# Key transposes of the next chunk moved into the visit of the chunk before it

## The chip, the cores and the metric

The program runs on one core of one Trainium2 chip. The metric is the device time of one execution in microseconds; a kernel's time is the median of its runs, and less is better.

## The reference

A gated linear attention (4 batches, 8 heads, 768 positions, 48 channels a head) feeds two feed-forward layers over its 3072 rows of 384 channels. All is float32.

```python
f = 1.0 / (1.0 + np.exp(-f_logit))
for t in range(S):
    state = f[:, :, t, :, None] * state + np.einsum('bhd,bhe->bhde', k[:, :, t], v[:, :, t])
    y[:, :, t] = np.einsum('bhd,bhde->bhe', q[:, :, t], state)
# x: y as 3072 rows of 384 channels
h = np.maximum(x @ w_in, 0.0);  x = h * h @ w_out
h = x @ w_in2;  out = np.where(h > 0, h, np.exp(np.minimum(h, 0)) - 1) @ w_out2
```

## The kernel before

**Chunks.** The attention is cut into 24 chunks: 128 positions of one batch, chunk g being of batch g % 4. Within a chunk the recurrence is replaced by matmuls: running products of the gates (two scans on VectorE, DVE) scale q and k, products of q and k give scores inside the chunk, and a state per batch carries what came before. Four chunks make a block of 512 rows, the unit of the feed-forward layers.

**Slots.** The two layers have 6 blocks each with 16 slices of the hidden width, so 192 units. The program is recorded in slots: in slot u TensorE (PE) gets `up(u)`, nine matmuls of 512 columns into one bank, and `down(u - 2)`, nine matmuls of 512 columns into three banks `y`; `between(u)` gives ScalarE (ACT) and DVE the activation of unit u (on ACT `r` and `gg`, on DVE `gh`), and `low(u)` gives GpSimd (POOL) the subtraction `gl` of 128x512 that follows `gh`. What `down` reads was made nearly two slots earlier. Every 16 slots a block ends: one slot later (slots 33, 49, 65) its three `y` banks are copied out, two of them by DVE and one by ACT.

**Steps of a chunk.** A plan hands each step of chunk g to a slot, and the steps of a slot are recorded ahead of that slot's `up`. Each engine works its own queue strictly in that order. `NEAR[g]` is the slot of chunk g's visit: 19, 21, 23, 25 for chunks 8 to 11, then 28, 32, 36, and so on to 72 for chunk 23. The steps:

- `load_f`, `load_qk`: DMAs from the SP queue of the gates, and of k and q;
- `a_gate`: a tanh on ACT, then a scaling on POOL, on 112x521 gates;
- `a_decay`: on DVE a memset, two scans with a reciprocal between them and a minimum (`mn`); on POOL two operations of 112x4 (`wc`, and up to chunk 19 `dlast`);
- `a_scale`: on DVE q, then k, are multiplied by the products, in place (112x512 each);
- `a_keys`: four PE transposes of k (128x112 outputs) into the bank `a2`; `a_transposed`: ACT copies them to SBUF as `kt`;
- the visit: `a_far(g - 1)` (32 small matmuls of q with the states into the two banks of outputs `a0` and `a1`), `a_near(g)` (64 small matmuls), `a_out(g - 1)` (32 more into the banks of outputs, and ACT's copies of them), then on DVE `a_mask` and `a_states`;
- `a_rows`, `a_hi`, `a_lo`: six small DMAs, then a copy on ACT and the subtraction `xl` on DVE, that make the layer's input of it.

From slot 28 on the weights of the second layer are decoded beside this, once in four slots: in the slot after a visit an ACT copy `dec` and three DVE operations on 128x768 (L58, L61, L62), three slots later a split on ACT and DVE.

The step slots of chunk g were tied to its own visit:

```python
a = NEAR[g]
d = a - (4 if g <= 3 * B else 6)        # B = 4
at(d - 2, load_f, g);  at(d, load_qk, g);  at(d, a_gate, g)
at(d + 1, a_decay, g); at(d + 2, a_scale, g)
for h in (a_keys, a_transposed):
    at(a - (1 if g <= 3 * B else 2), h, g)
```

So for chunk 19, visited in slot 56: gates in slot 50, scans in 51, scaling in 52, transposes in 54.

Of the kernel before, what the change touches and what calls it, by code (L numbers as in the profile page):

```python
# [11 lines left out]
F32 = mybir.dt.float32  # L12
# [5 lines left out]
AF = mybir.ActivationFunctionType  # L18
# [3 lines left out]
B, H, S, D = 4, 8, 768, 48  # L22
NT, DM, DFF = B * S, H * D, 2048
NG = NT // 128
# [3 lines left out]
NP = H // 2  # L28
ROWS = 112
# [11 lines left out]
NEAR = dict(zip(range(B, NG), (5, 7, 9, 11, 19, 21, 23, 25, *range(28, 4 * NG - 23, 4))))  # L41
# [42 lines left out]
def chunked(ctx, tc, ff, qk, vk, vz, wraw, mask, ident, flag, out):  # L84
# [7 lines left out]
    V, A, G, PE = nc.vector, nc.scalar, nc.gpsimd, nc.tensor  # L92

    one = ctx.enter_context(tc.tile_pool(name="one", bufs=1))
# [7 lines left out]
    ps_a = ctx.enter_context(tc.tile_pool(name="ps_a", bufs=1, space=PSUM))  # L102

    idt = one.tile([128, 128], F32, name="idt")
# [18 lines left out]
    st = {}  # L123
# [82 lines left out]
    def a_keys(g):  # L206
        k = st[g]["k"].rearrange("r (p t) -> r p t", p=NP)
        st[g]["tp"] = tp = ps_a.tile([128, NP, 128], F32, tag="a2", name=f"tp{g}")
        for p in range(NP):
            PE.transpose(tp[:, p, 0:ROWS], k[:, p], idt[:ROWS, :ROWS])  # L210

    def a_scores(g):
        s = st[g]
        a_keys(g)
        q, k = (s[n].rearrange("r (p t) -> r p t", p=NP) for n in "qk")
        pool, tags = (ps_h, "hh") if g % 2 else (ps_y, ("y0", "y1"))
        s["sc"] = sc = [pool.tile([128, NP, 128], F32, tag=tags[j], name=f"sc{g}_{j}") for j in range(2)]
        for p in range(NP):
            for j, (lo, hi) in enumerate(HD):
                PE.matmul(sc[j][:, p], k[lo:hi, p], q[lo:hi, p], start=True, stop=True)  # L220
# [63 lines left out]
    def a_far(g):  # L284


        s = st[g]
        q = s["q"].rearrange("r (p t) -> r p t", p=NP)
        s["o"] = o = [ps_a.tile([128, NP, 64], F32, tag=f"a{c}", name=f"o{g}_{c}") for c in range(2)]
        for p in range(NP):  # L290
            for j, n in QUARTERS:
                c = j ^ n
                lo, hi = HD[j]
                PE.matmul(  # L294
                    o[c][64 * n:64 * n + 48, p], (s0, s1)[c][lo:hi, p], q[lo:hi, p, 64 - 64 * c:128 - 64 * c],
                    start=p == 0, stop=False, skip_group_check=True,
                )

        seen = one.tile([128, 2, NP], F32, tag="seen", name=f"seen{g}")
        for c in range(2):  # L300
            A.activation(seen[64:112, c], o[c][64:112, :, 0], AF.Copy)
# [252 lines left out]
    def at(slot, f, *args, to=plan):  # L554

        if slot > 1:
            to.setdefault(slot, []).append((f, args))
# [2 lines left out]
        at(f - 5, load_raw, 0, f)  # L560
    for g in range(B, NG):
        a = NEAR[g]
        d = a - (4 if g <= 3 * B else 6)
        at(d - 2, load_f, g)
        at(d, load_qk, g)
        at(d, a_gate, g)
        at(d + 1, a_decay, g)
        at(d + 2, a_scale, g)
        for h in (a_keys, a_transposed):
            at(a - (1 if g <= 3 * B else 2), h, g)  # L570
        at(d + 1 if g < B + 2 else max(d + 1, NEAR[g - 1] + 1), load_v, g)
        over = g > B and g != 2 * B
        if over:
            at(a, a_far, g - 1)
        at(a, a_near, g)
        if over:
            at(a, a_out, g - 1)
            at(a + 1, a_rows, g - 1)
        at(a, a_mask, g)
        at(a, a_states, g)  # L580
        if g in (2 * B - 1, NG - 1):
            for h in (a_far, a_out):
                at(a + 2, h, g)
            at(a + 3, a_rows, g)
            for h in (a_hi, a_lo):
                at(a + 4, h, g, to=behind)
        else:
            for h in (a_hi, a_lo):
                at(NEAR[g + 1] + 3, h, g)
# [21 lines left out]
    with tc.manual_schedule():  # L611
# [8 lines left out]
        for _ in range(3):  # L620
# [4 lines left out]
            "T": lambda: [nc.sync.dma_start(out=tri[c:c + 64], in_=mask[c:c + 64, 64 - c:128 - c]) for c in (0, 64)],  # L625
            "f": load_f, "q": load_qk, "v": load_v, "r": lambda f: load_raw(0, f),
            "g": a_gate, "d": a_decay, "c": a_scale, "s": a_scores, "t": a_transposed, "m": a_mask, "k": a_state,
            "y": a_direct, "h": a_hi, "l": a_lo,
            "x": a_whole, "b": begin_weights, "w": finish_weights, "C": store_weights,
# [113 lines left out]
@with_exitstack  # L743
def gated_attention_moe(ctx: ExitStack, tc: tile.TileContext, ff, qk, vk, vz, nat, wraw, mask, ident, out):
    pool = ctx.enter_context(tc.tile_pool(name="flag", bufs=1))
    flag = pool.tile([1, 1], I32, name="flag")
    with ExitStack() as inner:
        chunked(inner, tc, ff, qk, vk, vz, wraw, mask, ident, flag, out)
    rv = tc.nc.values_load(flag[0:1, 0:1], min_val=0, max_val=1)
    with tc.If(rv == 1):  # L750
        with ExitStack() as inner:
            general(inner, tc, nat, wraw, ident, out)
# [58 lines left out]
```

## Time and profile before

| | |
|---|---|
| median of 3 runs | 887.52 us (886.96 to 887.74) |
| the profiled execution | 887.76 us, of it 886.0 us span |
| PE busy | 871.9 us, 98% of the span, 6240 matmuls |
| DVE busy | 552.8 us, 62% |
| ACT busy | 454.1 us, 51% |
| POOL busy | 280.7 us, 32% |
| chain of work that ended last | PE 96%, its lines L533 and L469 44% each |
| line of the transposes (L210) in that chain | 1% |

The span is that of the one execution that was profiled; 1.8 us of that execution's time lie outside it. Shares of busy time are means over stages that differ: the first 30 us are the start, up to 480 us the first layer runs with the attention beside it, then the second layer alone. A row of a view by time gives the start in us from the span's start, the duration, the engine, the source line, the operation, and output<-inputs with sizes; "x4" merges equal neighbours, and then the duration is that of all of them.

### The profile page before, as it was taken

The numbers are of one execution on the slowest core, as the hardware profiler recorded it, in microseconds if no ns is written. First come the engines' busy times: TensorE is split into PE (matmuls) and PEld (weight loads), VectorE is DVE, ScalarE is ACT, GpSimd is POOL, SyncE is SP. The second block draws the span as 40 slices with busy tenths as digits, with TensorE's granted clock in tenths as the row PEclk, the third lists the DMA queues.
The fourth block names the chain that finished last, engine by engine and source line by source line (L and its number), as shares of the span: only waits on it lengthen the run. The fifth ranks groups of instructions, "written<-read, shape, count | busy, mean of one in ns | idle before, by whom it ended". The sixth has DMA issues, their size and how long they took to land.

```text
span 886.0 us, 15946 instructions
## 1 busy us (share of the span) xinstructions
PE 871.9 (98%) x6240; PEld 699.8 (79%) x6240; DVE 552.8 (62%) x841; ACT 454.1 (51%) x816; POOL 280.7 (32%) x244
## 2 busy tenths in 40 slices
PE   7999999999999999999999999999999999999996
PEld 5566678888888888888888888888888888888885
DVE  8997578888677777654431555555655654664543
ACT  4877745555544555544544444444544544444543
POOL 2120045443334232322333232333323232332321
PEclk8999999999999999999999999999999999999999
DMA  9994321335444343513686300100100200100001
GB/s 261 351 302 163 101 90 49 118 106 161 147 156 153 115 151 117 182 47 123 229 299 238 131 13 1 59 13 1 60 12 1 66 7 14 58 1 35 2 0 40
DMA packets 36516, 92.40 MB, mean 104 GB/s; under 512 B 5809, under 2 KB 12977, under 8 KB 36433
## 3 DMA queue, kind: packets, MB, share of 16 engines
q1 hardware_dynamic: 36288, 91.18, 30.9%
q8 instruction: 50, 0.82, 0.4%
q14 instruction: 34, 0.27, 0.1%
q10 hardware_dynamic: 144, 0.13, 0.0%
HBM read 64.55 MB, written 22.02 MB: 98 GB/s over the span
## 4 chain that ended last, share of the span: by engine, by line
PE 96%; DVE 1%; DMA 1%; ACT 1%; SPq 0%; issue 0%; ACTq 0%; DVEq 0%
PE y L533 44%; PE ph L469 44%; PE o L294 1%; PE o L309 1%; PE tp L210 1%; PE sk_a L233 1%; DMA vz<-vz 1%; PE yp L278 1%; PE sk_a L242 1%; PE sc L220 0%; PE sk_h L242 0%; PE ph L458 0%; PE sk_h L233 0%; PE kv L268 0%; DVE t L502 0%
## 5 line engine op out<-in xcount | busy, mean ns | idle before, releaser
L516 POOL TENSOR_TENSOR gl<-gg,gh 128x512 fp32r<-128x512 f32 x175 | 233.7, 1336 | 471.4 <-PE ph L469 191.8
L533 PE MATMUL y<-gh,wf 128*128 128x512 f32 (+1 forms) x582 | 178.0, 387 | 0.3 <-ACT yo L545 0.3
L502 DVE SCALAR_TENSOR_TENSOR t<-r,t 128x512 f32<-128x512 f32 (+1 forms) x97 | 72.3, 745 | 154.8 <-ACT r L501 154.6
L498 ACT ACTIVATE r<-ph 128x512 f32<-128x512 f32 (+1 forms) x97 | 57.8, 596 | 181.5 <-PE ph L469 176.6
L469 PE MATMUL ph<-xh,w 128*128 128x512 f32 x558 | 149.7, 403 | 0.8 <-DVE w L430 0.8
L533 PE MATMUL y<-gh,w 128*128 128x512 f32 x480 | 147.8, 389 | 0.0
L469 PE MATMUL ph<-xh,wf 128*128 128x512 f32 (+1 forms) x582 | 146.4, 387 | 0.0
L533 PEld LDWEIGHTS y<-gh,wf 128*128 128x128 f32 x582 | 108.8, 188 | 22.8 <-ACT yo L545 0.5
L469 PEld LDWEIGHTS ph<-xh,wf 128*128 128x128 f32 x582 | 108.6, 188 | 22.3
L469 PEld LDWEIGHTS ph<-xh,w 128*128 128x128 f32 x558 | 101.4, 188 | 24.8 <-DVE w L430 1.4
L533 PE MATMUL y<-gl,wf 128*128 128x512 f32 (+1 forms) x291 | 112.5, 387 | 0.0
L533 PEld LDWEIGHTS y<-gh,w 128*128 128x128 f32 x480 | 90.1, 188 | 18.8
L490 ACT ACTIVATE r<-ph 128x512 f32<-128x512 f32 x80 | 47.8, 598 | 105.8 <-PE ph L469 88.5
L533 PE MATMUL y<-gl,w 128*128 128x512 f32 x240 | 93.4, 389 | 0.0
L469 PE MATMUL ph<-xl,wf 128*128 128x512 f32 (+1 forms) x291 | 81.1, 387 | 0.0
L469 PE MATMUL ph<-xl,w 128*128 128x512 f32 x279 | 78.5, 389 | 0.0
L503 DVE SCALAR_TENSOR_TENSOR gg<-ph,t 128x512 f32<-128x512 f32 (+1 forms) x97 | 66.6, 686 | 10.4 <-DVE t L502 0.5
L496 DVE TENSOR_TENSOR gh<-r 128x512 fp32r<-128x512 f32 x64 | 44.1, 688 | 45.2 <-ACT r L490 44.7
L533 PEld LDWEIGHTS y<-gl,wf 128*128 128x128 f32 x291 | 54.6, 188 | 11.1
L469 PEld LDWEIGHTS ph<-xl,wf 128*128 128x128 f32 x291 | 54.3, 188 | 11.1
L500 ACT ACTIVATE t<-r 128x512 f32<-128x512 f32 (+1 forms) x97 | 61.0, 629 | 3.1
L501 ACT ACTIVATE r<-r 128x512 f32<-128x512 f32 (+1 forms) x97 | 60.9, 628 | 3.1
(110 smaller groups left out, 1054.7 us busy)
## 6 DMA issues: line engine op xcount, KB each, us to landing
raw<-wraw SPq DMA_DIRECT2D x32, 768.0 KB, 6.9
wst<-w SPq DMA_DIRECT2D x16, 768.0 KB, 3.4
wf<-wst SPq DMA_DIRECT2D x16, 768.0 KB, 4.7
ff<-ff SPq DMA_DIRECT2D x22, 227.9 KB, 6.3
k<-qk SPq DMA_DIRECT2D x22, 224.0 KB, 3.4
q<-qk SPq DMA_DIRECT2D x22, 224.0 KB, 4.5
x2d<-yo SPq DMA_DIRECT2D x18, 256.0 KB, 2.7
x<-x2d SPq DMA_DIRECT2D x18, 256.0 KB, 3.0
```

Source lines behind the costliest of these rows:

```text
L210: PE.transpose(tp[:, p, 0:ROWS], k[:, p], idt[:ROWS, :ROWS])
L233: PE.matmul(sc[j][64 * c:64 * c + 64, p], k[lo:hi, p, 64 * c:64 * c + 64], q[lo:hi, p, 64 - 64 * c:128 - 64 * c], start=True, stop=True,)
L469: PE.matmul(ph, w[:, a, 0, 128 * k:128 * k + 128], b[:, k, c], start=(m == 0), stop=(m == len(todo) - 1))
L490: A.activation(r[:, c], ph, AF.Relu)
L496: V.tensor_tensor(out=gh[:, c], in0=r[:, c], in1=r[:, c], op=ALU.mult)
L498: A.activation(r[:, c], ph, AF.Relu, scale=-1.0)
L500: A.activation(t[:, c], r[:, c], AF.Tanh, scale=-0.5)
L501: A.activation(r[:, c], r[:, c], AF.Exp, scale=-1.0)
L502: V.scalar_tensor_tensor(out=t[:, c], in0=r[:, c], scalar=1.0, in1=t[:, c], op0=ALU.add, op1=ALU.mult)
L503: V.scalar_tensor_tensor(out=gg[:, c], in0=ph, scalar=0.0, in1=t[:, c], op0=ALU.max, op1=ALU.add)
L516: G.tensor_tensor(out=gl, in0=gg, in1=gh, op=ALU.subtract)
L533: PE.matmul(yp_[i][m][:, c], w[:, 128 * m:128 * m + 128], b[:, c], start=(f == 0 and n_ == 0), stop=(f == NF - 1 and n_ == len(terms) - 1) ...
```

## The change

For chunks 12 to 23 the transposes of k move from two slots ahead of the chunk's own visit (chunk 12: one slot) to the front of the visit of the chunk before it. They are written not to the bank `a2` but to the columns 256 to 479 of the two banks of outputs, which that visit fills in columns 0 to 255. ACT's copy `kt` becomes two copies of half the width, one slot after that visit. The other steps are now tied to that earlier visit: with d = NEAR[g - 1] - 3 the gates are worked in slot d, the scans in d + 1, the scaling in d + 2, in the slot ahead of the transposes. For chunks 13 to 23 each of these comes one slot earlier than before, for chunk 12 two slots. Chunk 19 now has its gates in slot 49, its scans in 50, its scaling in 51 and its transposes in 52. The loads of v, the visits and all feed-forward work keep their slots.

```diff
+    def a_keys_ahead(g):
+        k = st[g]["k"].rearrange("r (p t) -> r p t", p=NP)
+        st[g - 2]["oo"] = oo = [ps_a.tile([128, 512], F32, tag=f"a{c}", name=f"o{g - 2}_{c}") for c in range(2)]
+        st[g]["tp"] = tp = [o[:, 256:480].rearrange("r (p t) -> r p t", p=2) for o in oo]
+        for p in range(NP):
+            PE.transpose(tp[p // 2][:, p % 2], k[:, p], idt[:ROWS, :ROWS])
+
+    def a_transposed_ahead(g):
+        st[g]["kt"] = kt = one.tile([128, NP, ROWS], F32, tag="kt", name=f"kt{g}")
+        for c in range(2):
+            A.activation(kt[:, 2 * c:2 * c + 2], st[g]["tp"][c], AF.Copy)
...
     def a_far(g):
-        s["o"] = o = [ps_a.tile([128, NP, 64], F32, tag=f"a{c}", name=f"o{g}_{c}") for c in range(2)]
+        if "oo" in s:
+            o = [i[:, 0:256].rearrange("r (p t) -> r p t", p=NP) for i in s["oo"]]
+        else:
+            o = [ps_a.tile([128, NP, 64], F32, tag=f"a{c}", name=f"o{g}_{c}") for c in range(2)]
+        s["o"] = o
...
-        d = a - (4 if g <= 3 * B else 6)
+        ahead = g >= 3 * B
+        d = NEAR[g - 1] - 3 if ahead else a - 4
...
-        for h in (a_keys, a_transposed):
-            at(a - (1 if g <= 3 * B else 2), h, g)
+        if ahead:
+            at(d + 4, a_transposed_ahead, g)
+        else:
+            for h in (a_keys, a_transposed):
+                at(a - 1, h, g)
...
+        if g + 1 < NG and g + 1 >= 3 * B:
+            at(a, a_keys_ahead, g + 1)
         if over:
             at(a, a_far, g - 1)
```

PE, chunk 19. Before, the end of slot 53 and the begin of slot 54 (`y3_...` is `down`, `ph3_6` is `up`, `tp19` the transposes):

```order
L533 MATMUL y3_1_3449<-gh3_3_3501,w0_3_457 128x512 x2
L533 MATMUL y3_1_3449<-gl3_3_3502,w0_3_457 128x512
L533 MATMUL y3_2_3450<-gh3_3_3501,w0_3_457 128x512 x2
L533 MATMUL y3_2_3450<-gl3_3_3502,w0_3_457 128x512
L210 MATMUL tp19_3665<-idt_85,k19_3433 128x112 x4
L469 MATMUL ph3_6_0_3678<-xh3_2514,w0_6_612 128x512 x6
L469 MATMUL ph3_6_0_3678<-xl3_2515,w0_6_612 128x512 x3
```

After, the end of slot 51 and the begin of the visit of slot 52 (`o17_0` and `o17_1` are the two banks of outputs, the rows with `q17` are `a_far(17)`):

```order
L550 MATMUL y3_1_3457<-gl3_1_3431,w0_1_416 128x512
L550 MATMUL y3_2_3458<-gh3_1_3430,w0_1_416 128x512 x2
L550 MATMUL y3_2_3458<-gl3_1_3431,w0_1_416 128x512
L218 MATMUL o17_0_3513<-idt_85,k19_3392 128x112 x2
L218 MATMUL o17_1_3514<-idt_85,k19_3392 128x112 x2
L311 MATMUL o17_0_3513<-q17_2921,s0_97 48x64 x2
L311 MATMUL o17_1_3514<-q17_2921,s1_98 48x64 x2
```

The transposes stand between the last matmul of one slot and the first small matmuls of the visit, two slots earlier.

DVE, from the copies of a finished block in slot 49 on (`gh3_1` belongs to slot 49, `gh3_2` to 50, `gh3_3` to 51; `ds1` are the products of chunk 19, and masks with `sk18` belong to the visit of slot 52). Before:

```order
L547 COPY yo2_0_3408<-y2_0_2494 128x512
L547 COPY yo2_2_3414<-y2_2_2496 128x512
L496 TENSOR_TENSOR gh3_1_3417<-r3_1_3419 128x512
L496 TENSOR_TENSOR gh3_2_3460<-r3_2_3462 128x512
L358 TENSOR_TENSOR xl4_3469<-x1_16_3331,xh4_3468 128x3x128
L179 MEMSET lim_87 112x9
L181 SCALAR_TENSOR_TENSOR ds1_91<-ff19_3343,lim_87 112x520
L182 RECIPROCAL lim_87<-ds1_91 112x8
L183 SCALAR_TENSOR_TENSOR ds1_91<-ff19_3343,lim_87 112x521
L186 TENSOR_TENSOR mn_88<-mn_88,ds1_91 112x8
L496 TENSOR_TENSOR gh3_3_3501<-r3_3_3503 128x512
L260 COPY_PREDICATED sd0_95<-tri_92,sk18_a2_3530 128x256
```

After:

```order
L564 COPY yo2_0_3421<-y2_0_2502 128x512
L564 COPY yo2_2_3427<-y2_2_2504 128x512
L513 TENSOR_TENSOR gh3_1_3430<-r3_1_3432 128x512
L179 MEMSET lim_87 112x9
L181 SCALAR_TENSOR_TENSOR ds1_91<-ff19_3233,lim_87 112x520
L182 RECIPROCAL lim_87<-ds1_91 112x8
L183 SCALAR_TENSOR_TENSOR ds1_91<-ff19_3233,lim_87 112x521
L186 TENSOR_TENSOR mn_88<-mn_88,ds1_91 112x8
L513 TENSOR_TENSOR gh3_2_3468<-r3_2_3470 128x512
L375 TENSOR_TENSOR xl4_3477<-x1_16_3339,xh4_3476 128x3x128
L204 TENSOR_TENSOR q19_3391<-q19_3391,ds1_91 112x512
L204 TENSOR_TENSOR k19_3392<-k19_3392,ds1_91 112x512
```

The scans stand behind `gh3_1` instead of behind `xl4`, and the scaling of chunk 19 stands ahead of the visit of slot 52 (it followed that visit's masks and states before).

ACT, slots 48 and 49 (`gg3_0` belongs to slot 48, `dec1_5` is the decode of slot 49, `ff19` the gates of chunk 19). Before:

```order
L490 ACTIVATE r3_0_3370<-ph3_0_0_3349 128x512
L491 ACTIVATE gg3_0_3371<-r3_0_3370 128x512
L56 ACTIVATE dec1_5_3384<-raw1_5_3231 128x768
L545 ACTIVATE yo2_1_3411<-y2_1_2495 128x512
L490 ACTIVATE r3_1_3419<-ph3_1_0_3389 128x512
L491 ACTIVATE gg3_1_3420<-r3_1_3419 128x512
L255 ACTIVATE kt18_3430<-tp18_3425 128x448
L172 ACTIVATE ff19_3343<-ff19_3343 112x521
```

After:

```order
L507 ACTIVATE r3_0_3374<-ph3_0_0_3353 128x512
L508 ACTIVATE gg3_0_3375<-r3_0_3374 128x512
L223 ACTIVATE kt18_3386<-o16_0_3264 128x224
L223 ACTIVATE kt18_3386<-o16_1_3265 128x224
L172 ACTIVATE ff19_3233<-ff19_3233 112x521
L56 ACTIVATE dec1_5_3397<-raw1_5_3235 128x768
L562 ACTIVATE yo2_1_3424<-y2_1_2503 128x512
L507 ACTIVATE r3_1_3432<-ph3_1_0_3402 128x512
L508 ACTIVATE gg3_1_3433<-r3_1_3432 128x512
```

Two half copies of `kt18` and the tanh of chunk 19 now stand ahead of `dec1_5`; before, `kt18` and the tanh followed `gg3_1`.

## Rows read from the trace of the kernel before

**Rows 1.** Waits of PE between 45 and 480 us: in total, times, longest.
```profile
PE o L309 <- ACT seen L301: 0.5, 2, 0.3
```

**Rows 2.** PE by time, slots 41 to 44: start, us, instructions of one row.
```profile
235.34 1.52 PE L469 MATMUL ph<-xh,w 128*128 128x512 f32 x6
...
239.42 0.55 PE L210 MATMUL tp<-idt,k 112*128 112x112 f32 x4
239.74 1.64 PE L469 MATMUL ph<-xh,w 128*128 128x512 f32 x6
...
243.94 1.52 PE L469 MATMUL ph<-xh,w 128*128 128x512 f32 x6
...
247.79 0.39 PE L533 MATMUL y<-gl,w 128*128 128x512 f32 x1
248.11 0.27 PE L294 MATMUL o<-q,s 48*48 48x64 f32 x4
```

**Rows 3.** PE by time, the start of the program at 23 us.
```profile
23.19 0.57 PE L210 MATMUL tp<-idt,qk 112*128 112x112 f32 x4 [0.40 <-PE kv L268]
23.69 0.38 PE L220 MATMUL sc<-qk 48*128 48x128 f32 x2
```

**Rows 4.** PE by time, first small matmuls of the visits in slots 25, 48, 52.
```profile
157.34 0.44 PE L294 MATMUL o<-q,s 48*48 48x64 f32 x16
...
267.06 0.44 PE L294 MATMUL o<-q,s 48*48 48x64 f32 x16
...
286.00 0.39 PE L294 MATMUL o<-q,s 48*48 48x64 f32 x12
```

**Rows 5.** ACT by time, slots 48 to 50.
```profile
272.69 0.89 ACT L56 ACTIVATE dec<-raw 128x768 f32<-128x768 f32 x1
...
278.55 0.53 ACT L255 ACTIVATE kt<-tp 128x448 f32<-128x448 f32 x1
278.97 0.63 ACT L172 ACTIVATE ff<-ff 112x521 f32<-112x521 f32 x1
```

**Rows 6.** POOL by time, slots 48 to 50.
```profile
273.33 1.30 POOL L516 TENSOR_TENSOR gl<-gg,gh 128x512 fp32r<-128x512 f32 x1 [3.93 <-DVE gh L496]
...
280.28 0.64 POOL L173 TENSOR_SCALAR ff<-ff 112x521 f32<-112x521 f32 x1
```

**Rows 7.** DVE by time, slots 48 and 49, to the last instruction of slot 49.
```profile
273.61 1.45 DVE L58 TENSOR_SCALAR dec<-dec 128x768 uint32<-128x768 uint32 x1 [0.44 <-ACT dec L56]
...
276.96 1.28 DVE L547 COPY yo<-y 128x512 f32<-128x512 f32 x2
278.16 0.68 DVE L496 TENSOR_TENSOR gh<-r 128x512 fp32r<-128x512 f32 x1
```

**Rows 8.** DVE by time, the scans of slot 22.
```profile
141.22 0.68 DVE L496 TENSOR_TENSOR gh<-r 128x512 fp32r<-128x512 f32 x1
...
145.40 0.14 DVE L186 TENSOR_TENSOR mn<-mn,ds 112x8 f32<-112x8 f32 x1
```

**Rows 9.** POOL by time, beside those scans.
```profile
142.08 2.30 POOL L516 TENSOR_TENSOR gl<-gg,gh 128x512 fp32r<-128x512 f32 x1 [1.18 <-DVE lim L179]
...
145.53 1.13 POOL L194 COPY dlast<-ds 112x4 f32<-112x4 f32 x1
```

**Rows 10.** DVE by time, slots 23 to 26.
```profile
150.51 0.68 DVE L204 TENSOR_TENSOR k<-k,ds 112x512 f32<-112x512 f32 x1
...
160.74 0.07 DVE L179 MEMSET lim<- 112x9 f32 x1
...
164.12 0.69 DVE L496 TENSOR_TENSOR gh<-r 128x512 fp32r<-128x512 f32 x1
...
165.79 1.81 DVE L204 TENSOR_TENSOR k<-k,ds 112x512 f32<-112x512 f32 x1
```

**Rows 11.** POOL by time, slot 26.
```profile
165.31 1.74 POOL L516 TENSOR_TENSOR gl<-gg,gh 128x512 fp32r<-128x512 f32 x1 [1.66 <-DVE xl L358]
```

**Rows 12.** The page on DMA issues: KB each, us to landing.
```profile
q<-qk SPq DMA_DIRECT2D x22, 224.0 KB, 4.5
```

## The prediction

> **What bounds the kernel now.** I read the page's busy shares first: PE is busy for 98% of the span. That alone would not say that PE is the limit in the part that changes, so the second view is what PE waited for while the first layer and the attention run side by side: between 45 and 480 us there is one kind of wait, 0.5 us in two places [rows 1]. In that stretch the time is the length of PE's queue, and everything else is hidden behind it. So there are two questions: how much shorter does PE's queue become, and does anything that was hidden until now make PE wait? For the second I followed DVE, ACT and POOL by time from one visit to the next, since the change asks for the scaled k earlier than before.
>
> **PE's queue.** What is removed: a slot without transposes takes 239.42 - 235.34 = 4.08 us, one with them 243.94 - 239.42 = 4.52 us [rows 2]. So four transposes on their own cost 0.44 us, 12 times 5.3 us. What is added: eighteen matmuls in 4.08 us are 0.23 us each, and the first transpose starts 0.23 us after the last matmul ahead of it. Today the first small matmul of a visit starts 248.11 - 247.79 = 0.32 us after it [rows 2]. How long four transposes take ahead of small matmuls is seen only in the start of the program, where they go ahead of small matmuls of another shape: 23.69 - 23.19 = 0.50 us [rows 3]. Then a visit takes 0.23 + 0.50 - 0.32 = 0.41 us more, 12 times 4.9 us. The bounds: if the transposes ran into what follows as quickly as into a large matmul, 239.74 - 239.42 = 0.32 us [rows 2], a visit would take 0.23 more; at most it takes the 0.44 that they cost alone. So PE's queue changes by -2.5 to 0 us. I take the 0.50, as those rows too are transposes ahead of small matmuls: **-0.4 us**. The move as such hardly pays, because the array still streams the same four transposes.
>
> **What is asked for earlier.** Until now k of a chunk was scaled two slots ahead of its transposes. Now the scaling is in the slot just ahead of them, and the transposes stand at the head of a visit, so that all of the visit and the `up` behind it wait in PE's queue if k is late. I work out for three kinds of visit when DVE has k ready and when PE is due.
>
> *Visits after a block's end (slots 36, 52, 68).* Take slot 52, whose matmuls started at 286.00; its PE queue loses 0.44 (the transposes of slot 50) and the transposes start 0.09 sooner than the small matmuls did (0.32 - 0.23), so PE is due at 285.47 by the clock of this trace [rows 2, 4]. DVE's chain, from the visit of slot 48 on, which starts at 267.06 [rows 4]:
> - ACT: two half copies `kt` and the tanh now stand ahead of `dec`. The tanh takes 0.63; a full copy 0.53, so two halves between 0.53 and 1.06; `dec` ended at 272.69 + 0.89 = 273.58 and will end between 274.7 and 275.3 [rows 5].
> - POOL: `gl` runs from 273.33 to 274.63, then comes the gate's scaling of 0.64, to 275.27 [rows 6].
> - DVE's first decode operation was held by that `gl`: it ended at 275.06, 0.43 after `gl`, where it started at 273.61 [rows 6, 7]. I expect it behind the gate's scaling in the same way: 275.27 + 0.43 = 275.70, 0.64 later than before. The rest of the decode and the two block copies follow unchanged, so `gh` of slot 49, which started at 278.16 [rows 7], starts at 278.80.
> - Now the scans come directly behind `gh`. The same order stands in slot 22 of this trace: from `gh` at 141.22 to the end of `mn` at 145.40 + 0.14 it took 4.32 us, with POOL's `gl` in between, which took 2.30 instead of 1.30 [rows 6, 8, 9]. So the next `gh` starts at 283.12.
> - Then `gh`, `xl`, q, k. That order stands in slot 26: `gh` started at 164.12 and k ended at 165.79 + 1.81 = 167.60, 3.48 us [rows 10]. k alone takes 0.68; the other 1.13 us are `gl`, which got in between q and k [rows 10, 11]. k is ready at 283.12 + 3.48 = 286.60, and PE waits 286.60 - 285.47 = **1.1 us**. If `gl` stays behind k, k is ready at 285.47, and PE waits for nothing: the bounds are 0 and 1.1 us.
>
> Which of them? In slots 52 and 36 `dlast` stands ahead of `gl` on POOL; in slot 22 `dlast`, a copy of four columns, was held for 1.13 us from 145.53 on [rows 9], until two DVE instructions that started later were over. If it is held so again, `gl` comes behind k. No row decides it, and I take the middle, 0.55 each. Chunk 23 has no `dlast`: in slot 68 `gl` is asked for at once, as in slot 26, and I take 1.1. Together 2.2 us.
>
> [...]
>
> *Other visits of the decode stage (slots 40, 44, 48, 56, 60, 64).* The same chain without the block copies: DVE gets to `gh` 1.2 us sooner (278.16 - 276.96, [rows 7]), k is ready at 285.40 by the clock used above, against 285.47. No wait, but with 0.07 us to spare. Slot 32 has more DVE work than these and no block copies; I take 0 and count up to 1.1 in the range.
>
> *The visit of slot 25.* Chunk 12 is now scaled in slot 24, and visits are two slots apart there. Behind k of chunk 11, which started at 150.51 and after which DVE is free 0.60 later, come the scans, a split, `gh`, `xl`, q, k: the very sequence that began at 160.74 and ended at 167.60, 6.86 us [rows 10]. So k is ready at 157.97. PE is due at 157.34 - 0.09 = 157.25 [rows 4]: a wait of **0.7 us**, and none if `gl` stays behind k. I take 0.7, as it is the same sequence and chunk 12's `dlast` is not behind a held scan there. Slot 28 has three slots from the visit before it instead of two, and as no decode stands ahead of its scans I take 0 there.
>
> **Edits at nothing.** The two half copies on ACT release nothing that PE needs for four slots. Moving the loads one slot up the SP queue: only that of chunk 12 meets a wait, as its buffer is read in slot 23; behind it on SP are q, gates and rows not needed before slot 24, and q lands in 4.5 us [rows 12], well within the slot and a half that is left. `gl`, `gh` and the `y` banks have nearly a slot of slack; if that cover were gone, PE would wait in `down`, not at a visit.
>
> **The sum.** The profiled execution took 887.76, of it 886.0 span. -0.4 + 0.7 + 2.2 = +2.5 gives 890.3 on it. That execution is 0.24 above the median of 887.52, so the forecast for the median is **890.0 us**. A change under 0.2% (1.8 us) can't be told from none in this kernel.
>
> **The rivals.**
> 1. *POOL stays behind DVE* (not slower). If DVE runs `gh`, `xl`, q, k without a gap, all waits vanish: 887.5 - 0.4 = 887.1. For it: the held `dlast`; against it: the k of 1.81 us. With slot 25 or slot 68 alone it lies between 887.1 and 889.3. It decides from the point where k is ready before PE is due, 1.1 us before the estimate of slot 52.
> 2. *DVE is later than worked out*, by 0.3 us, say, because a half copy costs more or the decode is held twice. Then the six regular visits wait 0.2 each, slot 32 up to 1.1, and the three visits after a block take the full 1.1 + 0.3: 887.5 - 0.4 + 0.7 + 4.2 + 1.2 + 0.7 = 893.9 at most, some 892 to 894.
> 3. *The transposes flow into the small matmuls* as into a large one, and k is in time: 887.5 - 2.5 = 885.0.
>
> **How the numbers follow.** Forecast, 889.3 to 891.5: 0.42. Rival 1 in full, no wait anywhere: 0.20; in part, up to 889.3: 0.20. Rival 2: 0.12. Rival 3: 0.06. The forecast and rival 2 are slower, 0.54; rival 1 in both forms lies within 0.2%, 0.40; rival 3 is faster, 0.06. The range leaves out rival 3 and the upper half of rival 2: 886.6 to 892.8.
>
> **What would show it.** On PE: from slot 25 on no transposes but those ahead of small matmuls, with about 0.50 us to the first of these, and in the view of waits a new line, transposes waiting for the scaling of k (L204): some 0.7 us in slot 25, up to 1.1 in slots 36, 52 and 68, next to nothing elsewhere. On POOL: `gl` between q and k of the same chunk. The forecast is wrong if that line is missing or under 1 us in total, if k is done well ahead in slot 52, or if PE waits for something else, the `y` banks above all.

## The result, and the profile after

The changed kernel takes 895.43 us (895.13 to 896.42), the kernel before 887.6: a ratio of 1.0092 (95% interval 1.0079 to 1.0105). It is slower, as forecast, but by 7.8 us instead of 2.5, and outside the range. The profiled execution took 895.52 us, of it 893.6 us span.

The waits of TensorE in the stretch of [rows 1], which had one line, are now (columns: in total, times, longest):

```profile
PE o L218 <- issue: 2.1, 2, 1.1
PE o L218 <- PE y L550: 1.4, 2, 0.9
PE o L326 <- issue: 1.0, 1, 1.0
PE o L218 <- DVE k L204: 0.9, 1, 0.9
PE o L326 <- ACT seen L318: 0.5, 2, 0.3
```

L218 is the line of the moved transposes. Its three rows are one and the same wait, in slots 25, 32, 36, 52 and 68: each of these five groups of transposes starts 0.10 to 0.26 us after DVE's k has ended, and only the name of the releaser differs. The row of L326 with "issue" is something else, a gap inside the output matmuls of slot 25, and was not foreseen.

The view by time of slots 50 to 52, where [rows 6 to 8] stood for the estimate (DVE, POOL and the last matmul rows of PE; brackets give the idle time of the engine before a row and what ended it, "issue" where the profile shows nothing that it waited for):

```profile
287.79 0.68 DVE L513 TENSOR_TENSOR gh<-r 128x512 fp32r<-128x512 f32 x1
287.86 1.13 POOL L194 COPY dlast<-ds 112x4 f32<-112x4 f32 x1
...
288.39 0.55 DVE L375 TENSOR_TENSOR xl<-x,xh 128x384 fp32r<-128x384 f32 x1
...
288.86 1.95 DVE L204 TENSOR_TENSOR q<-q,ds 112x512 f32<-112x512 f32 x1
...
288.95 1.31 POOL L533 TENSOR_TENSOR gl<-gg,gh 128x512 fp32r<-128x512 f32 x1
...
290.04 0.39 PE L550 MATMUL y<-gl,w 128*128 128x512 f32 x1
290.73 0.68 DVE L204 TENSOR_TENSOR k<-k,ds 112x512 f32<-112x512 f32 x1
...
291.51 0.57 PE L218 MATMUL o<-idt,k 112*128 112x112 f32 x4 [1.09 <-issue]
```

`dlast`, 0.19 us at its shortest in this trace, takes 1.13 here: it is held through `gh` and `xl`. Then `gl` starts, and q, which needs 0.68 us alone, takes 1.95 and ends 0.55 after `gl`. From `gh` to the end of k it is 291.41 - 287.79 = 3.62 us; the forecast had 3.48. The last matmul of `y` started at 290.04, so PE was due at 290.27 and waited 1.24 us. (The view shows less, 1.09, as it counts from the matmul's modelled end.) In the same way the waits are 1.01 us in slot 25, 0.17 in 28, 0.66 in 32, 1.21 in 36 and 1.09 in 68, 5.4 us in all. In the other visits k is ready 0.1 to 0.2 us ahead of time; in slot 40, for instance, the transposes follow at once:

```profile
233.15 0.39 PE L550 MATMUL y<-gl,w 128*128 128x512 f32 x1
233.40 0.57 PE L218 MATMUL o<-idt,k 112*128 112x112 f32 x4
233.90 0.32 PE L311 MATMUL o<-q,s 48*48 48x64 f32 x6
```

Those three rows also show the 0.50 us from transposes to small matmuls that was taken from [rows 3]. The gap of slot 25, and the last matmul of the program:

```profile
157.10 0.39 PE L550 MATMUL y<-gl,w 128*128 128x512 f32 x1
158.34 0.58 PE L218 MATMUL o<-idt,k 112*128 112x112 f32 x4 [0.85 <-DVE k L204]
...
160.25 0.61 PE L326 MATMUL o<-sd,vk 64*48 64x64 f32 x25
161.88 0.32 PE L326 MATMUL o<-sd,vk 64*48 64x64 f32 x5 [1.02 <-issue]
...
885.71 0.28 PE L550 MATMUL y<-gl,wf 128*128 128x256 f32 x1
```

From the start of that last matmul to the end of the span it is 893.6 - 885.71 = 7.89 us; in the kernel before it was 6.87:

```profile
879.13 0.28 PE L533 MATMUL y<-gl,wf 128*128 128x256 f32 x1
```

So the 7.6 us of span come to this: 5.4 the waits for k, 1.3 the gap in slot 25 (that visit grew by 2.7, of which 1.0 is the wait and 0.4 the transposes), 1.0 the end of the program, and -0.1 the rest.

### The profile page after: what moved, and what is told of

Same layout as the page of the kernel before. It is cut to its first block, busy times and chain, and to the rows that moved or that the text cites. A ratio compares the mean times of both kernels' runs of the same rounds, so it can differ in the third digit from the quotient of the medians.

```text
span 893.6 us, 15950 instructions
## 1 busy us (share of the span) xinstructions
PE 873.8 (98%) x6240; PEld 702.1 (79%) x6240; DVE 552.8 (62%) x841; ACT 454.3 (51%) x828; POOL 297.4 (33%) x244
## 4 chain that ended last, share of the span: by engine, by line
PE 94%; DVE 1%; ACT 1%; issue 1%; DMA 1%; SPq 0%; ACTq 0%; DVEq 0%
PE y L550 44%; PE ph L486 43%; PE o L311 1%; PE o L326 1%; PE sk_a L246 1%; PE yp L291 1%; DMA f<-ff 1%; PE o L218 1%; PE tp L210 1%; PE sk_a L255 1%; PE sc L233 0%; PE sk_h L255 0%; PE ph L475 0%; DMA x<-x 0%; PE kv L281 0%
## 5 line engine op out<-in xcount | busy, mean ns | idle before, releaser
L533 POOL TENSOR_TENSOR gl<-gg,gh 128x512 fp32r<-128x512 f32 x175 | 244.1, 1395 | 474.8 <-PE ph L486 203.3
L486 PEld LDWEIGHTS ph<-xl,w 128*128 128x128 f32 x279 | 52.4, 188 | 11.2
```

Source lines behind the costliest of these rows:

```text
L486: PE.matmul(ph, w[:, a, 0, 128 * k:128 * k + 128], b[:, k, c], start=(m == 0), stop=(m == len(todo) - 1))
L533: G.tensor_tensor(out=gl, in0=gg, in1=gh, op=ALU.subtract)
```

## The experiments

Each kernel is the changed kernel with the edit shown, unless it is said to be the kernel before. "PE's row" below means the start of the last matmul, from the view by time; the end is what follows it.

### The late k and POOL's subtraction

**k ahead of q** in `a_scale`.

```diff
-        for o, first, apart in ((0, 66, 456), (1, 0, 588)):
+        for o, first, apart in ((0, 66, 456), (1, 0, 588))[::-1 if g >= 3 * B else 1]:
```

> The changed kernel with one edit: from chunk 12 on DVE scales k first and q second. PE's, ACT's, POOL's and SP's instructions stay as they are. Theory A (PE waits because the scaled k is late on DVE): k ends 0.6 us sooner where POOL's subtraction runs ahead of q (slots 25, 32, 36, 52, 68) and 1.7 us sooner in slot 28, so the waits ahead of the transposes fall from 5.4 us in all to about 2.2 (0.4 in slot 25, 0.6, 0.6 and 0.5 in slots 36, 52, 68) and the time from 895.4 to about 892. Theory B (the wait comes from sharing the two banks of outputs, or from the transposes standing ahead of the small matmuls): no change, 895.4. The gap of 1.2 us among the small matmuls of slot 25: if it follows from the wait for k it shrinks or goes (then about 891), if it hangs on the instructions' places alone it stays. The last microsecond at the end of the program: stays if it hangs on SP's instructions' places.

Measured 891.9 us, ratio 1.0050 (1.0033 to 1.0066). The rows of slot 52, and the waits of PE:

```profile
286.23 1.94 DVE L204 TENSOR_TENSOR k<-k,ds 112x512 f32<-112x512 f32 x1
...
286.31 1.30 POOL L533 TENSOR_TENSOR gl<-gg,gh 128x512 fp32r<-128x512 f32 x1
...
288.27 0.57 PE L218 MATMUL o<-idt,k 112*128 112x112 f32 x4 [0.48 <-PE y L550]
```

```profile
PE o L218 <- PE y L550: 1.5, 4, 0.5
PE o L326 <- issue: 1.0, 1, 1.0
```

Now it is k that `gl` holds up, 1.94 us, but k is one instruction further forward, and each wait is about 0.6 us shorter. Nothing else was touched: 3.5 us come back by that alone, of them 3.2 in these waits. The gap in slot 25 stays.

**The subtraction left out.** POOL writes zeros instead of `gl` in units 22 to 68, so the outputs lack the share of that low part; PE's matmuls with it stay.

```diff
-            G.tensor_tensor(out=gl, in0=gg, in1=gh, op=ALU.subtract)
+            if 22 <= 16 * i + f <= 68:
+                G.memset(gl.bitcast(F32), 0.0)
+            else:
+                G.tensor_tensor(out=gl, in0=gg, in1=gh, op=ALU.subtract)
```

> The changed kernel, but in slots 22 to 68 POOL's subtraction of the 128x512 activations (the low part of the split) is left out: a memset of the same tile stands in its place, which reads nothing, so the low parts are zero there. Theory A with POOL's subtraction as the cause: k is ready 2 us and more sooner (1.1 us in front of k, 0.7 to 1.0 us in the scans), no wait for k anywhere, 5.4 us less, and 6.6 less if the gap in slot 25 goes too: 889 to 890. If DVE is late by its own work alone, or by the banks: waits of 1 us stay in slots 36, 52 and 68, about 893 to 895.

Measured 889.37 us. Of the waits only the gap is left, beside the one that the kernel before has too:

```profile
PE o L326 <- issue: 1.1, 1, 1.1
```

Without POOL's subtraction no transposes wait for k anywhere, though scans, q and k stand where the change put them.

**The same in two units only**, those whose `gl` lies over q ahead of slots 36 and 52.

```diff
-            G.tensor_tensor(out=gl, in0=gg, in1=gh, op=ALU.subtract)
+            if 16 * i + f in (34, 50):
+                G.memset(gl.bitcast(F32), 0.0)
+            else:
+                G.tensor_tensor(out=gl, in0=gg, in1=gh, op=ALU.subtract)
```

> The changed kernel without the low part's subtraction on POOL in two units, those whose subtraction lay over the scaling of q ahead of slots 36 and 52 (that low part is zero, so the outputs lack that share). [...]

Measured 893.36 us; 895.4 less the two waits of 1.21 and 1.24 us would be 893.0. In slot 36 the wait is gone (transposes 0.23 us behind the last matmul, at 214.04). In slot 52 0.76 of the 1.24 us stay, as q now waits for its load:

```profile
289.12 0.69 DVE L204 TENSOR_TENSOR q<-q,ds 112x512 f32<-112x512 f32 x1 [0.73 <-DMA q<-qk]
289.73 0.69 DVE L204 TENSOR_TENSOR k<-k,ds 112x512 f32<-112x512 f32 x1
```

So for slot 36 the subtraction is the whole wait. For slot 52 this run alone doesn't decide it: the load of q, issued on SP behind rows of x, landed 6.3 us after its issue and was the next thing to be late. In the run without any of these subtractions that visit has no wait, and k is ready 0.65 us ahead. (The profiled execution took 894.6 us, 1.2 above the median, so that wait need not be in all of them.)

**The earlier steps alone.** Loads, gates, scans and scaling as in the changed kernel, the transposes and their copy in their old slots and bank.

```diff
-            at(d + 4, a_transposed_ahead, g)
+            for h in (a_keys, a_transposed):
+                at(a - (1 if g == 3 * B else 2), h, g)
...
-        if g + 1 < NG and g + 1 >= 3 * B:
-            at(a, a_keys_ahead, g + 1)
```

> The steps of chunks 12 to 23 (loads, gates, scans, scaling) in their new, earlier slots, but the transposes in their old slots and in the old bank. Theory A: k is ready two slots ahead of need, PE waits for nothing, time of the kernel before, 887.6, up to 1.1 more if the end of the program is longer here too. A rival, that the earlier scans and gates themselves cost (POOL and DVE in each other's way, late activations or late copies of a block): 889 to 895, with PE waiting in the large matmuls.

Measured 888.98 us, ratio 1.0016 (1.0006 to 1.0026); in the stretch of [rows 1] PE waits for the same 0.5 us as there. DVE and POOL hinder each other as in the changed kernel (q takes up to 1.94 us), but PE needs k only two slots later. Of the 1.5 us that are left the end of the program is 1.1 (see below), and in the profiled execution 0.5 lay in the first 29 us, ahead of everything that differs. So the earlier steps and the collision by themselves cost PE nothing.

### Sooner steps move the collision

**All steps of chunks 12 to 23 one slot sooner.**

```diff
-        d = NEAR[g - 1] - 3 if ahead else a - 4
+        d = NEAR[g - 1] - 4 if ahead else a - 4
...
-            at(d + 4, a_transposed_ahead, g)
+            at(d + 5, a_transposed_ahead, g)
```

> The changed kernel with the loads, gates, scans and scaling of chunks 12 to 23 one more slot earlier; the transposes stay at the head of the visit. Theory A: k is ready a slot ahead, no wait for k, and as the transposes themselves cost in a visit about what they cost alone, the time is that of the kernel before, 887 to 888, plus up to 1.1 us at the end of the program; without the wait for k the gap in slot 25 goes as well if it follows from it (if not, 1.2 more). Theory B (banks or place of the transposes): PE still waits ahead of the transposes, about 895.

Measured 902.37 us, a miss by 14. No transposes wait any more (k is ready 2.8 us ahead in the decode stage), but PE waits elsewhere:

```profile
PE sk_a L255 <- DMA vk<-vk: 9.2, 2, 7.6
PE y L550 <- DVE yo L564: 2.8, 3, 0.9
```

The first row lies in slots 21 and 23. On SP the load of chunk 12's gates had come ahead of a load of vk. It waits for a buffer that DVE's scans still read (the view of SP's waits names DVE's L183, 6.4 us at the longest), and all behind it waits too; SP by time, first here, then in the changed kernel:

```profile
127.64 8.09 SPq L135 DMA_DIRECT2D ff<-ff  x2
135.78 0.42 SPq L161 DMA_DIRECT2D vk<-vk  x1
```

```profile
127.61 1.97 SPq L135 DMA_DIRECT2D ff<-ff  x1
129.62 0.42 SPq L161 DMA_DIRECT2D vk<-vk  x1
```

vk is issued 6.2 us later, and the loads behind it too. By PE's rows 13.6 us are lost by the end of slot 24. Part of that is slower matmuls after the waits, in which TensorE stood still for 1.6 and 7.6 us: behind the second, six matmuls of 512 columns take 2.93 us (from 160.76 on), where such rows in [rows 2] take 1.52 and 1.64. The mean granted clock of this execution is 0.986, that of the changed kernel's 0.993. The second row of the waits lies in slots 34, 50 and 66:

```profile
216.88 0.96 DVE L62 SCALAR_TENSOR_TENSOR dec<-raw,dec 128x768 uint32<-128x768 uint32 x1
217.75 1.28 DVE L564 COPY yo<-y 128x512 f32<-128x512 f32 x2
218.49 0.74 PE L550 MATMUL y<-gh,w 128*128 128x512 f32 x2 [0.94 <-DVE yo L564]
```

The scans now stand ahead of the decode and of the copies of the block's outputs, and the `y` banks come free 0.9 us late.

**The same from chunk 13 on, gate loads left in their slots.**

```diff
-        d = NEAR[g - 1] - 3 if ahead else a - 4
-        at(d - 2, load_f, g)
+        d = NEAR[g - 1] - (4 if g > 3 * B else 3) if ahead else a - 4
+        at(d - (1 if g > 3 * B else 2), load_f, g)
...
-            at(d + 4, a_transposed_ahead, g)
+            at(NEAR[g - 1] + 1, a_transposed_ahead, g)
```

> The changed kernel with the q and k loads, the gate, the scans and the scaling of chunks 13 to 23 one slot sooner again; the load of the gate's input stays in its slot, and chunk 12 is as in the changed kernel. Theory A (TensorE is held only by the late k): the waits ahead of the transposes at slots 28, 32, 36, 52 and 68 go (0.17 + 0.66 + 1.21 + 1.24 + 1.09 = 4.4 us), and 895.4 becomes 891.0. Rival B (VectorE is full in the slots around a block's end, and whatever is put there makes something else late): the scans then lie in slots 33, 49 and 65, where the copies of the block's outputs out of PSUM are due, and y waits some 0.9 us for them at slots 34, 50 and 66, as in the run before: 4.4 less and 3 x 0.9 to 1.1 more, 893.7 to 894.3. If the 13.6 us lost before slot 24 in that run came from the load of the gate's input standing in the sync queue ahead of vk, they don't come back here.

Measured 893.4 us.

```profile
PE y L550 <- DVE yo L564: 2.8, 3, 0.9
PE o L326 <- issue: 1.3, 1, 1.3
PE o L218 <- DVE k L204: 1.3, 1, 1.3
```

The 13.6 us are not there. This run puts both chunk 12's steps and the gate loads back; that it was the load is read from SP's rows above. The waits at slots 28 to 68 are gone and the `y` banks have taken their place, as rival B said; chunk 12's wait in slot 25 grew to 1.4. PE's row is only 0.8 us better than the changed kernel's; the other 1.3 of the 2.0 us gained are a shorter end (6.7 us against 7.9).

**From chunk 13 on, otherwise as changed.**

```diff
-        ahead = g >= 3 * B
+        ahead = g > 3 * B
...
-        if g + 1 < NG and g + 1 >= 3 * B:
+        if g + 1 < NG and g + 1 > 3 * B:
```

> The changed kernel with the new order from chunk 13 on instead of chunk 12, so that slot 25 carries no transposes and the instructions ahead of its output matmuls are as many as in the kernel before. Theory A with F (the late k of chunk 12 costs 1.0 us there, and the place of the instruction block's end 1.2): both go, 895.4 - 2.2 - 0.1 = 893.1, with the waits at slots 28, 32, 36, 52 and 68 unchanged (4.4 us). Rival (the gap follows the first visit that carries transposes): a gap of about 1 us shows at slot 28, 894.2.

Measured 895.34 us instead of 893.1. The gap is gone, but the wait in slot 28 grew from 0.17 to 1.78 us and that of chunk 12's own transposes in slot 27 is 0.5:

```profile
PE o L218 <- issue: 3.7, 3, 1.6
PE o L218 <- PE y L550: 1.4, 2, 0.9
PE o L326 <- ACT seen L318: 0.5, 2, 0.3
PE tp L210 <- DVE lim L179: 0.5, 1, 0.5
```

Chunk 12 is back in slots 24 to 26, chunk 13 in 25 to 27: two chunks' scans follow each other on DVE. I had not seen that when I wrote the expectation.

### The gap in slot 25

**24 small matmuls more** among the warm-up ones, so that all later code of TensorE stands 48 instructions further back.

```diff
+        for _ in range(24):
+            PE.matmul(warm[:, 0:16], ss[0][:, 0, 0], ss[0][:, 0, 0, 0:16], start=True, stop=True)
```

> The changed kernel with 24 matmuls of 16 columns more among the warm-up ones at the start, in TensorE's idle time there (1.76 us); every later TensorE instruction then stands 48 instructions further back in the program. Theory F (the gap of 1.0 to 1.2 us in the middle of slot 25's output matmuls comes from where a 16 KB block of instructions ends): the gap leaves that place, moves some 24 matmuls up or vanishes; if it vanishes 894.3, if it moves 895.4. Rival V (the visit's own work makes it): the gap stays ahead of the last 7 matmuls of that visit, 895.4. The waits for k stay as they are under both.

Measured 899.64 us. PE by time, the added matmuls and slot 25:

```profile
7.29 7.67 PE L646 MATMUL warm<-ss 128*128 128x16 f32 x48
...
163.77 0.58 PE L218 MATMUL o<-idt,k 112*128 112x112 f32 x4 [0.85 <-DVE k L204]
...
165.68 0.63 PE L326 MATMUL o<-sd,vk 64*48 64x64 f32 x30
166.24 1.64 PE L486 MATMUL ph<-xh,w 128*128 128x512 f32 x6
```

The 24 matmuls cost 7.67 us where I had counted on 1.8 of idle time, which delays all that follows by 5.4. In slot 25 the wait for k is the same 1.01 us, and the gap has vanished: that visit is 1.3 us shorter than in the changed kernel. With the same visit and the same wait, but the code in another place, there is no gap; the visit's work alone doesn't make it. Nor, it seems, does the place alone: in the run with all steps one slot sooner as many matmuls stand ahead of that visit as in the changed kernel, k of chunk 12 is ready 5.7 us ahead, and slot 25 has no gap. That is one run, in which TensorE also stood still for 9.2 us in slots 21 and 23, so the part that k plays is less sure than that of the place.

### The end of the program

**Two needless loads on SP**, in the kernel before.

```diff
+    for u in (80, 81):
+        at(u, lambda: nc.sync.dma_start(out=idt, in_=ident))
```

> The kernel before with two needless loads of the identity by SyncE in slots 80 and 81, when nothing uses it. From the last matmul to the end of the program it took 6.8 us in the kernel before, 7.9 in the changed one, and 6.25 to 8.3 in the experiments so far. Theory T (that stretch hangs on where SyncE's code ends, and not on the change): it changes by some tenths up to 1.6 us here, and the time with it, 887 to 888.6. Rival: it stays 6.8 us and the time 887.5.

Measured 887.57 us, the end 7.0 us against 6.9: it moved by a tenth, and this run alone tells nothing. It suggested what to count, though: kernels with 548 SP instructions in their trace had ends of 7.9 to 8.4 us, those with 554 to 558 had 6.3 to 7.0.

**Six needless loads on SP**, in the changed kernel (the same lines with `range(80, 86)`; 555 SP instructions).

> The changed kernel with six needless loads of the identity by SyncE in slots 80 to 85. So far the stretch from the start of the last matmul to the end was 7.9 to 8.35 us in the seven kernels whose trace has 548 SyncE instructions, and 6.25 to 6.95 us in the four that have 554 to 558; the long ones have a gap of 1.4 to 1.7 us among SyncE's last instructions, the short ones none. Theory T (that stretch hangs on how many instructions SyncE has, so on where its code ends in a block of instructions): with some 8 more it is 6.3 to 7.0 us without the gap, and 895.4 becomes 894.2 to 894.5. Rival (the changed order itself makes it): it stays 7.9 and the time 895.4. The waits for k stay.

Measured 894.45 us. The last matmul starts at 886.06 and the span ends at 892.5:

```profile
886.06 0.28 PE L550 MATMUL y<-gl,wf 128*128 128x256 f32 x1
```

The end is 6.4 us instead of 7.9, and the gap of 1.4 us that the changed kernel has among SP's closing semaphore instructions is not there; of these 1.5 us 0.4 are lost again, because one small matmul that reads the identity waited for one of the loads, so these were not quite needless. The longer end goes with how much code SP has, not with what the change does to PE; why it does, no run shows.

### A version without the losses

**Mended:** from chunk 13 on, k ahead of q (both edits as above), and `gl` on VectorE in the three units where it lay over q ahead of slots 36, 52 and 68.

```diff
...
-            G.tensor_tensor(out=gl, in0=gg, in1=gh, op=ALU.subtract)
+            (V if 16 * i + f in (34, 50, 66) else G).tensor_tensor(out=gl, in0=gg, in1=gh, op=ALU.subtract)
```

> The run from chunk 13 on, with k scaled ahead of q, and with the low part's subtraction in the units whose subtraction lies over the scaling of q ahead of slots 36, 52 and 68 done by VectorE instead of POOL. Theory A: no wait ahead of the transposes is longer than 0.2 us, and TensorE's row is the kernel before's less 0.04 to 0.05 us per visit, 0.4 in all: 887.1 with the end of the kernel before, 888.2 to 888.6 with the longer end that most variants show. Rival B (VectorE is full there and something else comes late, the gh of the next unit or the copies of the block's outputs): y or ph wait 0.5 to 1 us at three places, 889 to 891. Under either nothing here makes the kernel faster than before by more than 0.05%.

Measured 890.1 us, above the 888.2 to 888.6 of theory A; ratio 1.0031 (1.0020 to 1.0042). No transposes of a visit wait over 0.16 us. PE's row is 0.7 us above the kernel before's (0.9 counted from 29 us on): 0.5 for the transposes of slot 27 and 0.6 for five waits of 0.09 to 0.16 ahead of the visits' transposes, less what the move gains. The end has 8.1 us.

**Level:** the mended run, chunk 12's steps one slot sooner, and the six SP loads.

```diff
...
-        d = NEAR[g - 1] - 3 if ahead else a - 4
+        d = NEAR[g - 1] - 3 if ahead else a - (5 if g == 3 * B else 4)
...
```

> The mended run with two edits more: the gate, scans and scaling of chunk 12, which keeps its old transposes in slot 27, one slot sooner, so that they no longer stand right ahead of chunk 13's (there the transposes of slot 27 waited 0.5 us), and the six needless SyncE loads. Theory A with T: the 0.5 us and the 1.2 us of the end go, and TensorE's row ends within 0.5 us of the kernel before's: 888.4 is the upper end, 887.4 to 888.0 the middle. Rival B (VectorE is full there too): some other wait of 0.5 us or more takes the place, 888.5 to 889.

Measured 887.72 us against 887.65 for the kernel before, ratio 1.0002 (0.9992 to 1.0011). In the stretch of [rows 1] PE waits for one thing, as before the change:

```profile
PE o L326 <- ACT seen L318: 0.5, 2, 0.3
```

Four waits of 0.04 to 0.17 us ahead of visits' transposes are left, too short for that view. PE's row is 0.2 us above the kernel before's and the end 0.3 below it. With nearly all losses taken away the moved transposes gain nothing that can be measured. No version here beats the kernel before.

## Why the prediction was right in direction and wrong in size

| term | forecast, us | measured, us |
|---|---|---|
| PE's queue, 12 visits | -0.4 | -0.1; -0.2 to -0.7 in four other kernels |
| wait, slot 25 | 0.7 | 1.01 |
| waits, slots 28 and 32 | 0 | 0.17 + 0.66 |
| waits, slots 36 and 52 | 0.55 each | 1.21 and 1.24 |
| wait, slot 68 | 1.1 | 1.09 |
| gap in slot 25 | none | 1.3 |
| end of the program | none | 1.0 |

*PE's queue* was right. A visit with transposes is 0.4 us longer, a slot without them 0.4 shorter; what is left of PE's row in the runs with k first, without the subtraction, mended and level, when their waits and the gap are taken off, lies on both sides of -0.4. Rival 3 is out, as the transposes take 0.50 us ahead of small matmuls.

*DVE's chain to slot 52* was right to a tenth: by the forecast k is ready 1.1 us after PE is due, if `gl` comes ahead of q; it came 1.14 after, and the transposes 0.10 behind it.

*The step that failed* is "No row decides it, and I take the middle, 0.55 each". `dlast` was held, as in slot 22, and from that I let `gl` fall behind k half of the time. In fact, in slots 36 and 52, `dlast` ends within 0.05 us of `xl`, and `gl` behind it starts at once and is over 0.54 and 0.55 us before q: waits of 1.21 and 1.24 us. The row of slot 22 was also read wrongly. `dlast` starts there at 145.53 and ends at 146.66; of the two DVE instructions that it was held through only the second starts later:

```profile
145.46 0.55 DVE L430 TENSOR_TENSOR w<-w 128x384 fp32r<-128x384 f32 x1
145.93 0.68 DVE L496 TENSOR_TENSOR gh<-r 128x512 fp32r<-128x512 f32 x1
```

After them DVE has nothing to do until 148.19, so that row could not show whether the `gl` behind `dlast` gets in ahead of a DVE instruction that waits. With `gl` in at all three visits, the upper bound that the prediction worked out for slot 52, the price would have been 1.1 us each, near the 1.21, 1.24 and 1.09 measured. The order of the starts does not tell which of two instructions is held: in slot 52 `dlast` starts at 287.86 and `xl` at 288.39, yet `xl` takes its usual 0.55 us and `dlast` lasts 1.13, until `xl` is over. (The starts of q and `gl` there, 0.09 apart, decide nothing, as neighbouring rows of DVE overlap by 0.08.)

That step is 1.35 of the 5.1 us by which the span came out above the forecast of +2.5. The rest are terms that were set to nothing or too low: 0.66 and 0.17 the waits in slots 32 and 28, 0.3 that in slot 25, 1.3 the gap, 1.0 the end and 0.3 PE's queue. With full prices for slots 36 and 52 the forecast would have been 891.1, still too low. (Rival 2's "893.9 at most" counts slot 32 with 0.7 where it allows 1.1.)

*Slot 32* I set to 0 for want of a row, and left 1.1 to the range: 0.66. There a split of the weights stands on DVE ahead of `gh`, `xl`, q and k, and q takes 1.94 us beside `gl`, as in most visits. *Slot 25*: k came 0.75 us after PE was due, as worked out, but the transposes only 0.26 after k.

*Nothing in the prediction covered* the last two rows of the table, 2.3 us together. A few added instructions take either of them away: the gap goes with the place of PE's code, and, as far as one run shows, with the late k too; the end goes with the amount of SP's code. So 5.4 of the 7.6 us of span are the mechanism that was forecast, at nearly twice its size, and most of the rest hangs on how much code stands where.

*Edits at nothing* held in the changed kernel: neither the half copies nor the loads made PE wait. The cover was thinner than forecast, though. q's load was given 4.5 us and took 6.3 ahead of slot 52 in the run without two subtractions, where q waited 0.73 us for it. The `y` banks were given "nearly a slot of slack"; in the two runs with sooner steps it was used up, at 3 times 0.9 us.

## What to carry to other kernels

Before work that others wait for is moved to another place in an engine's queue, ask what runs beside it there on the engines that can hold it up: a subtraction of 1.3 us on POOL made q or k 0.6 to 1.3 us longer in eleven of twelve visits, and it cost time only where k had less slack than that. When a row leaves two outcomes open, one cheap and one dear, and an instruction is queued directly behind the held one, count the dear one. A step that is moved earlier to escape a wait meets the next tenant of that slot; here the copies of finished blocks, or a load ahead of another on one queue.

## What the runs showed of the hardware

In slot 25 TensorE stood for 1.0 to 1.3 us near the end of a burst of over a hundred small matmuls, ahead of the same matmul, in six kernels, in all of which k comes late or less than 0.4 us ahead there; it did not with the 24 matmuls put ahead, with k 5.7 us ahead, or without transposes in that slot. The traces of five kernels, the one before and the changed one among them, show a DMA queue of the kind "instruction" that moves 0.82 MB in 50 packets of 16 KB. I take it for TensorE's, an estimate from the counts: 12480 matmuls and weight loads are 250 to a packet. In the changed kernel the twelfth of these packets begins at 159.47, 1.1 us after the start of the transposes, and takes 0.96; the burst goes on at 161.88, 2.4 us after the packet's start. In the kernel before the twelfth begins at 156.22, 1.1 us ahead of the visit, and the burst has no gap. That the gap has to do with these packets is argued from these two traces and not shown; what the runs show is that the gap needs the place, and that it stayed away in the one run that had the place, the transposes and a k with slack.

The end of the program is the plainer case: 7.9 to 8.4 us with 548 SP instructions (eight kernels), 6.3 to 7.0 with 554 to 558 (six). In a kernel where 1.8 us can just be told from no change, that is up to two microseconds that go with the amount of code and not with the work, and a control with a few added instructions costs one run.
